# Exponentials added on GpSimd, w_out converted in three places, and a second MLP layer that gives rows

## The chip, the cores and the metric

The kernel runs on one core of a Trainium2 chip. A core has five engines that work side by side and wait for one another by semaphores: TensorE (PE, matrix products, with its weight loads shown as PEld), VectorE (DVE), ScalarE (ACT), GpSimd (POOL) and SyncE (SP), which here issues most of the DMAs. The metric is device time in microseconds; the kernel before takes 1161.94 us (median of 3 runs, 1161.27 to 1163.94).

## The reference

Three layers follow each other, for 1792 tokens of width 768:

```
attention: 4 batches x 12 heads, 448 positions, head width 64, q and k RMS-normalised;
           exp(scores - row max) / (row sum + 1e-9) @ v
routing:   logits = x @ w_gate; all 1792 x 8 pairs in descending order; a token goes to the first
           expert that still has room (224 tokens each); out = relu(x @ w1[e]) @ w2[e]
MLP:       h = x @ w_in (768 -> 2048); out = (h * cos(h)) @ w_out (2048 -> 768)
```

`w_in` and `w_out` arrive as float64 in DRAM; the kernel turns each value into two float32 parts (hi and lo) so that three fast products (hi*hi, hi*lo, lo*hi) keep the accuracy.

## The kernel before

**A planner sets the order.** The code does not issue instructions. It adds steps (engine, estimated cost, reads, writes) to a plan; `Plan.run` then simulates the engines with these costs and emits each engine's instructions in the order it found. So the order on each engine is fixed at build time, and an engine waits at an instruction whose input is late, whatever stands behind it.

**Attention** works on 24 pairs of heads. For a pair, `scores` makes the transposed scores in four chunks of 112 keys and two heads, ACT takes the exponential into `pf` (112 x 448), `weigh` multiplies them with v (`po`) and sums them over the keys by products with a column of ones (`dn`, 32 columns wide, in full float32), 8 tiles times 4 column groups per pair. POOL does part of the normalisation (`qn`, `rt`, `rs`) and a small copy (`mx`).

**Conversion of w_in and w_out** (`Narrow.piece`) takes one DMA in, one ACT operation, four DVE operations, one more ACT and one more DVE operation, and one DMA out. There are 32 pieces of w_in (384 elements a partition) and 24 of w_out (512 elements). `EARLY = 48` of the 56 are placed as filler under attention; the last 8 are converted straight into the weight tiles of the first MLP (`fresh`).

**Experts and MLP.** The router finds, expert by expert, which 224 tokens it gets (`phase`; a long chain of small DVE operations). The tokens are gathered by an indirect DMA (`xr`), transposed, and go through `expert`; w1 and w2 are split into hi and lo by ACT and DVE as they arrive. After two experts, `mlp` runs on their 448 tokens: the first layer makes 16 tiles of 128 features (`acc`), a cosine of six operations follows, and leaves `gh` and `gl`. The second layer makes six tiles of 128 outputs: the weights are stationary, the 448 tokens are the moving operand, 16 x 3 products each. Its result is transposed, so each tile is copied by ACT (`o`), turned back by four PE transposes (`tr`), copied by DVE into `xo`, and at the end four indirect DMAs of 112 rows put the rows where the index tile `idx` says. There are four such groups; the last splits its last tile in two halves of 224 tokens.

Of the kernel before, what the change touches and what calls it, by code (L numbers as in the profile page):

```python
# [264 lines left out]
LAND = 7.0  # L265
# [4 lines left out]
class Narrow:  # L270

    WIDE = {"wi": 3, "wo": 4}

    def __init__(self, nc, pairs):

        self.nc = nc
        self.todo, self.at = [], {}
        for tag, src, dst in pairs:
            s = src.bitcast(I32)
            for f in range(dst.shape[0]):  # L280
                n = self.WIDE[tag]
                for k in range(0, dst.shape[2], n):
                    w = s[k * 128:(k + n) * 128, f * 256:(f + 1) * 256].rearrange("(k p) c -> p k c", p=128)
                    self.at[tag, f, k] = len(self.todo)
                    self.todo.append((w, dst[f, :, k:k + n], f"{tag}{f}:{k}"))

    def piece(self, plan, i, raw, mag, parts=None):
# [3 lines left out]
        n = dst.shape[1]  # L291
        r, a = raw[:, 0:n], mag[:, 0:n]
# [3 lines left out]
        plan.add([("SP", 0.46, lambda: nc.sync.dma_start(r, src))], [], [r], dma=0.36 * n, land=LAND)  # L296
# [7 lines left out]
        plan.add([("SP", 0.46, lambda: nc.sync.dma_start(dst, o.bitcast(F32)))], [o], [name], dma=0.36 * n)  # L304

    def plan(self, plan, pool, last):

        most = max(self.WIDE.values())
        raw = plan.ring(pool)("nr", 4, [128, most, 256], I32)
        mag = plan.ring(pool)("na", 2, [128, most, 128], I32)  # L310
        for i in range(last):
            self.piece(plan, i, raw(), mag())
# [20 lines left out]
NKQ = 5  # L333
XKA = 0
# [20 lines left out]
def attention(tc, P, R, ident, q, k, v, g_q, g_k, w_gate, x_dram, L, other):  # L355
# [4 lines left out]
    with ExitStack() as ctx:  # L360
# [27 lines left out]
        pfs = ring("pf", NPF, [CP + 1, S])  # L388
# [40 lines left out]
        P.rush, pw = -1000.0, bd()  # L429
# [22 lines left out]
        for _ in range(NPF):  # L452
            zset(pfs()[96:CP + 1], 1.0)
# [87 lines left out]
        def scores(P_, a, z):  # L541

            k, q, t = keys[P_ % NKQ], queries[P_ % NKQ], shift_rows[P_ % 4]
            for c in range(a, z):
# [14 lines left out]
                for h in range(2):  # L559
                    pf = exps[P_, h, c] = pfs()  # L560
                    sc.activation(pf[0:CP], ps[h], AF.Exp)

        outs = {}

        def weigh(P_):
# [5 lines left out]
            for c0 in range(0, NC, 2):  # L571
                def both():
                    for c in range(c0, c0 + 2):
                        for h in range(2):
                            pe.matmul(po[h * D:(h + 1) * D], t[:, h, c], exps[P_, h, c][0:CP], start=c == 0,
                                      stop=c == NC - 1)

                block(both)
# [146 lines left out]
class Router:  # L725
# [3 lines left out]
    def __init__(self, nc, pool, ident, L, rows):  # L729
# [76 lines left out]
        v.tensor_copy(io, tmp[0:CP, 272:272 + CP])  # L806
        pc = t("pc", [CP, NCOL, 3], BF16)
# [237 lines left out]
    def phase(self, idx, eid, first, quick):  # L1045
# [52 lines left out]
        nc.rush = rush  # L1098

# [18 lines left out]

CP, E, CAP, DM, F1, F2 = 112, 8, 224, 768, 1024, 2048
# [10 lines left out]
TURN = 5  # L1130
# [5 lines left out]
def moe(tc, P, R, ident, x_rows, w1, w2, w_in, w_out, out, narrow):  # L1136

    nc = tc.nc
    with ExitStack() as ctx:
# [10 lines left out]
        rbuf = ring("r", 3, [128, PT])  # L1150
        kbuf = ring("k", 2, [128, PT], I32)
        obuf = ring("o", 1, [128, PT])
# [3 lines left out]
        xf = cst.tile([128, KD, CAP], F32, name="xf")  # L1156
        xo = cst.tile([CP, 4, DM], F32, name="xo")
        mags = ring("na", MAGS, [128, 4, 128], I32)
        x2h = cst.tile([128, KD, PT], F32R, name="x2h")
        x2l = cst.tile([128, KD, PT], F32R, name="x2l")  # L1160
        gh = cst.tile([128, K2, PT], F32R, name="gh")
        hT = gh[:, K1:K2]
        gl = cst.tile([128, K2, PT], F32R, name="gl")
# [5 lines left out]
        def route(t, behind):  # L1169
# [3 lines left out]
            R.phase(idx[t], eid[t], t == 0, t in QUICK)  # L1173
# [62 lines left out]
        def ready(src, k0, n, keys):  # L1236

            x = parts()[:, 0:n]
            P.add([("SP", 0.46, lambda: nc.sync.dma_start(x.bitcast(F32), src[:, k0:k0 + n]))], keys, [x],
                  dma=n * 0.35)  # L1240
            return x[:, :, 0], x[:, :, 1]

        def fresh(d, k0):
            x = parts()
            for k in range(k0, k0 + K1, 4):
                i = narrow.at["wo", d, k]
                if i >= EARLY:
                    raw = stage().rearrange("p k n -> p (k n)").bitcast(I32).rearrange("p (k n) -> p k n", k=4)
                    narrow.piece(P, i, raw, mags(), x[:, k - k0:k - k0 + 4])
# [54 lines left out]
        def mlp(grp, ahead):  # L1304
            w = len(grp) * CAP
            for f in range(K2):
                hi, lo = ready(w_in[f], 0, KD, [f"wi{f}:{k}" for k in range(0, KD, narrow.WIDE["wi"])])
                p = acc()[:, 0:w]
                for d in range(KD):
                    block(lambda: three(p, hi[:, d], lo[:, d], x2h[:, d, 0:w], x2l[:, d, 0:w], d == 0, d == KD - 1))  # L1310
                r, k, a = rbuf()[:, 0:w], kbuf()[:, 0:w], gh[:, f, 0:w]
# [7 lines left out]
                P.either("tensor_tensor", gl[:, f, 0:w], r, a.bitcast(F32), op=ALU.subtract)  # L1319
            for d in range(KD):  # L1320
                if grp is GROUPS[0] and narrow.at["wo", d, 0] >= EARLY:
                    both = [fresh(d, k0) for k0 in range(0, K2, K1)]
                else:
                    both = [ready(w_out[d], k0, K1, [f"wo{d}:{k}" for k in range(k0, k0 + K1, narrow.WIDE["wo"])])
                            for k0 in range(0, K2, K1)]
                last = d == KD - 1
                if d == TURN:
                    ahead()
                cut = w // 2 if last and grp is GROUPS[-1] else w
                for a in range(0, w, cut):  # L1330
                    n, z = cut // CP, slice(a, a + cut)
                    p = acc()[:, 0:cut]
                    for f in range(K2):
                        hi, lo = (x[:, f % K1] for x in both[f // K1])
                        block(lambda: three(p, hi, lo, gh[:, f, z], gl[:, f, z], f == 0, f == K2 - 1))
# [4 lines left out]
                    g0 = a // CP  # L1340
                    v.tensor_copy(xo[:, g0:g0 + n, d * 128:(d + 1) * 128],
                                  q[0:CP, 0:n * 128].rearrange("p (g c) -> p g c", g=n))
                    for g in range(g0, g0 + n) if last else ():
                        P.add([("POOL", 1.07, lambda g=g: scatter(xo[:, g], idx[grp[g // 2]][:, g % 2:g % 2 + 1]))],
                              [xo[:, g]], [], dma=0.96)
# [20 lines left out]

        fetch(0)
        for grp in GROUPS:
# [4 lines left out]
            behind = chain[-EARLIER]  # L1373
            mlp(grp, lambda: fetch(grp[-1] + 1, behind))
        P.run(zip(chain, chain[1:]), *TUNE_B)

EARLY = 48
# [3 lines left out]
def kernel(  # L1381
# [22 lines left out]
    w_out32 = dram.tile([KD, 128, F2 // 128, 2, 128], F32, name="w_out32")  # L1404
    narrow = Narrow(nc, [("wi", w_in, w_in32), ("wo", w_out, w_out32)])
# [35 lines left out]
```

## Time and profile before

| | |
|---|---|
| median of 3 runs | 1161.94 us |
| the profiled execution | 1161.31 us, of which the span is 1159.4 us |
| mean granted clock | 0.976 |
| PE, DVE, ACT, POOL busy | 96%, 77%, 56%, 12% |
| attention's last PE work | about 348 us into the span |
| first expert's first product | 384.8 us |

PE's busy time includes modelled ends of pipelined products, so it is not a measure of how full PE is. The rate is read from the starts of successive products, and which engine limits a stretch from its busy share there.

### The profile page before, as it was taken

To read this page: it belongs to the slowest core of one execution; us is meant where nothing else is said; L and a number is where in the kernel's file an instruction comes from. 1 tells how busy PE (TensorE), PEld (TensorE's weight loads), DVE (VectorE), ACT (ScalarE), POOL (GpSimd) and SP (SyncE) were. 2 spreads that over 40 slices of the span, in tenths; PEclk is the share of its full clock that TensorE was granted. 3 is DMA by queue.
4 is the path that set the end of the run, shared out by engine and by line. 5 is a ranking of instruction groups with operands and counts; after the bars stand their busy time and mean duration, and the time that the engine had idled before them with its cause. 6 is when DMAs were issued, how large, how long until landed. Compare 5 with 4: busy or idle time off the path is not lost.

```text
span 1159.4 us, 22182 instructions
## 1 busy us (share of the span) xinstructions
PE 1107.4 (96%) x7944; PEld 912.5 (79%) x7944; DVE 895.6 (77%) x2477; ACT 646.0 (56%) x1575; POOL 134.2 (12%) x288
## 2 busy tenths in 40 slices
PE   7999999999994999999999999999999999999996
PEld 4556666665553888999898899899899889999996
DVE  7878999999958888996997887578789577856401
ACT  4867888866552456763456564246666235746400
POOL 5432432331000000000001000001000000100001
PEclk9989999999995899999999999999999999999998
DMA  7236476565641489779579568838866956856761
GB/s 215 81 115 207 150 251 204 172 221 203 218 171 50 129 229 293 239 257 293 209 185 263 203 218 248 297 115 239 244 216 222 301 194 174 238 205 218 245 218 48
DMA packets 180814, 237.58 MB, mean 205 GB/s; under 512 B 14112, under 2 KB 156896, under 8 KB 175072
## 3 DMA queue, kind: packets, MB, share of 16 engines
q1 hardware_dynamic: 178144, 225.15, 61.4%
q0 software_dynamic: 2560, 11.01, 3.6%
q8 instruction: 62, 1.02, 0.4%
q14 instruction: 48, 0.39, 0.1%
HBM read 199.52 MB, written 36.52 MB: 204 GB/s over the span
## 4 chain that ended last, share of the span: by engine, by line
PE 36%; DVE 7%; DMA 6%; issue 1%; ACT 1%; SPq 0%; POOL 0%; POOLq 0%; ACTq 0%; DVEq 0%
PE acc L47 35%; DMA ws<-in_moe_w_dram 4%; DMA wx<-w_out 2%; DVE wx L47 2%; PE tr L47 1%; DVE r L47 1%; DVE oh L47 1%; ACT wx L1231 1%; DVE na L47 1%; DVE xo L47 0%; SPq L1014 0%; DMA rows<-vm 0%; DVE gl L47 0%; DVE xe L47 0%; POOL out_dram L1351 0%
## 5 line engine op out<-in xcount | busy, mean ns | idle before, releaser
L47 PE MATMUL acc<-gh,wx 128*128 128x448 f32 (+1 forms) x1568 | 360.7, 344 | 4.9 <-DVE gh L47 3.7
L47 PEld LDWEIGHTS acc<-gh,wx 128*128 128x128 f32 x1568 | 264.5, 189 | 23.5 <-DVE gh L47 6.0
L47 PE MATMUL acc<-x2h,wx 128*128 128x448 f32 x768 | 222.4, 368 | 0.0
L47 PEld LDWEIGHTS acc<-x2h,wx 128*128 128x128 f32 x768 | 144.7, 188 | 11.0
L47 PE MATMUL acc<-gl,wx 128*128 128x448 f32 (+1 forms) x400 | 143.2, 358 | 0.0
L47 PE MATMUL acc<-x2l,wx 128*128 128x448 f32 x384 | 140.3, 365 | 0.0
L47 DVE TENSOR_TENSOR wx<-ws,wx 128x768 fp32r<-128x768 f32 (+1 forms) x104 | 112.3, 1080 | 24.3 <-ACT wx L1231 22.1
L47 ACT ACTIVATE pf<-st 112x448 f32<-112x448 f32 x192 | 93.9, 539 | 50.4 <-PE st L47 49.8
L1231 ACT ACTIVATE wx<-ws 128x768 fp32r<-128x768 f32 (+1 forms) x104 | 97.7, 940 | 25.9 <-DMA ws<-in_moe_w_dram 14.0
L47 DVE TENSOR_REDUCE cm<-s 128x1 f32<-128x448 f32 x168 | 99.6, 618 | 12.5 <-PE s L47 10.1
L47 PE MATMUL acc<-xe,wx 128*128 128x448 f32 (+1 forms) x672 | 107.1, 320 | 0.5 <-DVE wx L47 0.5
L47 ACT ACTIVATE r<-r 128x448 f32<-128x448 f32 x128 | 74.1, 579 | 57.8 <-DVE r L47 56.0
L47 PEld LDWEIGHTS acc<-xe,wx 128*128 128x128 f32 x672 | 100.8, 189 | 5.4 <-DVE wx L47 0.8
L47 PE MATMUL st<-qq,kk 64*112 64x448 f32 x576 | 91.5, 397 | 1.9 <-ACT pf L47 1.9
L47 ACT ACTIVATE oh<-oh 128x896 bf16<-128x896 bf16 x48 | 45.6, 950 | 74.6 <-DVE oh L47 74.5
L1182 POOL DMA_INDIRECT xr<-x,idx x16 | 15.6, 977 | 588.1 <-issue 198.2
L47 PE MATMUL po<-pf,vr 112*64 112x448 f32 x384 | 83.1, 552 | 0.0
L47 PEld LDWEIGHTS acc<-gl,wx 128*128 128x128 f32 x400 | 75.5, 189 | 4.7
L47 PEld LDWEIGHTS acc<-x2l,wx 128*128 128x128 f32 x384 | 72.3, 188 | 5.2
L47 PEld LDWEIGHTS st<-qq,kk 64*112 64x112 f32 x576 | 49.3, 175 | 31.8 <-ACT pf L47 9.8
L47 ACT ACTIVATE sq<-qk 112x64 f32<-112x64 f32 (+1 forms) x195 | 57.2, 301 | 8.4 <-DVE rt L47 4.6
L47 DVE COPY xo<-tr 112x512 f32<-112x512 f32 (+1 forms) x25 | 16.6, 666 | 58.1 <-PE tr L47 56.4
(251 smaller groups left out, 1830.8 us busy)
## 6 DMA issues: line engine op xcount, KB each, us to landing
wx<-w_in SPq DMA_DIRECT2D x64, 768.0 KB
wx<-w_out SPq DMA_DIRECT2D x44, 1024.0 KB
ws<-in_moe_w_dram SPq DMA_DIRECT2D x64, 384.0 KB
ws<-in_moe_w_dram SPq DMA_DIRECT2D x48, 512.0 KB
nr<-in_moe_w_in_dram SPq DMA_DIRECT2D x32, 384.0 KB
w_in<-nr SPq DMA_DIRECT2D x32, 384.0 KB
nr<-in_moe_w_out_dram SPq DMA_DIRECT2D x16, 512.0 KB
w_out<-nr SPq DMA_DIRECT2D x16, 512.0 KB
```

Source lines behind the costliest of these rows:

```text
L47: self.plan.add([(self.eng, self.plan.cost(self.eng, name, out, r, kw), lambda: f(*args, **kw), self.plan.shares(self.eng, name, out, r, k ...
L1182: P.add([("POOL", 2.1 - 0.9 * h, lambda x=x, h=h: nc.gpsimd.indirect_dma_start(out=x, out_offset=None, in_=x_rows, in_offset=bass.Indirect ...
L1231: P.add([("ACT", 0.093 + n * 0.1067, lambda: nc.scalar.activation(hi, s, AF.Copy)), ("DVE", 0.07 + n * 0.0667, lambda: nc.vector.tensor_co ...
```

## The change

- After each pair of exponentials, POOL adds two neighbouring chunks into a new tile `pa`; the sums then use two tiles instead of four for each head. For the last pair only the first two chunks are added.
- `w_out` is stored in two layouts: 8 blocks of 256 rows by 512 columns, and 4 blocks of 512 rows by 256 columns. 38 pieces are converted under attention (`EARLY`), 6 after the first gather (`GAP`), into memory that is used later (`r`, `xo`), and 12 in the first MLP: the second half of every one of the 12 blocks. The first halves are loaded back from DRAM.
- The second layer has the tokens (`gh`, `gl`) as stationary operand, 128 at a time, and the weights as moving operand, 512 and then 256 columns wide. A group has 448 tokens; the first and third group do three tiles of 128 and leave 64 tokens, the second and fourth do four tiles with these 64. All three or four accumulators of a group are open at once. The result comes as rows: ACT writes it into `xo`, without transposes, and three or four indirect DMAs of 128 rows send it off.
- `place` moves the row indices into this division by products with a shifted identity.

```diff
-                    self.at[tag, f, k] = len(self.todo)
...
+                    tile = (b + 8 * (tag == "wo1")) % 3 if i else -1
+                    self.todo.append(((tag != "wi") * (1 + (i > 0) + (tile > 0)), (tag, b, i), (
+                        w.rearrange("(k p) c -> p k c", p=128), dst[b, :, i:i + n], f"{tag}{b}:{i}")))
+        self.todo.sort(key=lambda t: t[0])
...
+        def halved(P_, c):
+            if c and P_ == NPR - 1:
+                return
+            for h in range(2):
+                a = exps[P_, h, -1 - c] = pas()
+                P.gpsimd.tensor_tensor(a[0:CP], exps[P_, h, c], exps[P_, h, c + 1], op=ALU.add)
...
-                    for c in range(NC):
-                        n, e = CP + (c == 0), exps.pop((P_, h, c))
+                    halves = [c for c in (0, 2) if (P_, h, -1 - c) in exps]
+                    for c in range(0, NC, 2) if len(halves) == 2 else (0, 2, 3):
+                        n, e = CP + (c == 0), exps.pop((P_, h, -1 - c if c in halves else c))
...
-            for d in range(KD):
-                if grp is GROUPS[0] and narrow.at["wo", d, 0] >= EARLY:
-                    both = [fresh(d, k0) for k0 in range(0, K2, K1)]
...
-                    o, q = obuf()[:, 0:cut], turn()
-                    sc.activation(o, p, AF.Copy, scale=-1.0)
-                    for g in range(n):
-                        P.tensor.transpose(q[0:CP, g * 128:(g + 1) * 128], o[:, g * CP:(g + 1) * CP], ident)
...
+            starts, c0 = range(o, REST + PT - 64 * (1 - g % 2), 128), 0
+            for z, w in enumerate(w_out):
+                n, m = w.shape[2], w.shape[4]
+                ps = [acc()[:, 0:m] for _ in starts]
+                for k in range(0, K2, n):
+                    tag, b = f"wo{z}", k // n
+                    if g == 0 and narrow.late(tag, b, EARLY + GAP):
+                        hi, lo = fresh(w[b], tag, b)
+                    else:
+                        hi, lo = ready(w[b], narrow.keys(tag, b))
+                    if z and k == TURN:
+                        ahead()
+                    for s, p in zip(starts, ps):
+                        for i in range(n):
+                            f = k + i
+                            a, b = gh[:, f, s:s + 128], gl[:, f, s:s + 128]
...
+                                P.tensor.matmul(p, a, hi[:, i], start=f == 0, stop=False)
+                                P.tensor.matmul(p, b, hi[:, i], start=False, stop=False)
+                                P.tensor.matmul(p, a, lo[:, i], start=False, stop=f == K2 - 1)
...
         fetch(0)
+        gather = next(t for t in P.steps[n:] if t.ways[0][0] == "POOL" and t.dma)
+        for i in range(EARLY, EARLY + GAP):
+            n = len(P.steps)
+            narrow.piece(P, i, raws(), mags())
+            P.steps[n + 1].after[gather] = True
...
-EARLY = 48
+EARLY = 38
+GAP = 6
```

On PE, in the middle of attention, the sums of a pair (`dn`, each row four products) stood directly behind the pair's second half of `po`:

```order
L47 MATMUL po_223<-pf_199,vr_165 64x448
L47 MATMUL po_223<-pf_200,vr_165 64x448
L47 MATMUL dn_224<-pf_193,ones 32x112 x4
L47 MATMUL dn_224<-pf_195,ones 32x112 x4
L47 MATMUL dn_224<-pf_197,ones 32x112 x4
L47 MATMUL dn_224<-pf_199,ones 32x112 x4
L47 MATMUL dn_224<-pf_194,ones 32x112 x4
L47 MATMUL dn_224<-pf_196,ones 32x112 x4
L47 MATMUL dn_224<-pf_198,ones 32x112 x4
L47 MATMUL dn_224<-pf_200,ones 32x112 x4
```

In the same place of the changed kernel a block of eight score products and one more stand between them:

```order
L47 MATMUL st_231<-qq_151,kk_146 112x448
L47 MATMUL st_230<-sr_158,heads 112x448
L47 MATMUL st_231<-sr_158,heads 112x448
L47 MATMUL s_229<-kk_147,qq_152 128x448
L47 MATMUL dn_233<-pa_210,ones 32x112 x4
L47 MATMUL dn_233<-pa_206,ones 32x112 x4
L47 MATMUL dn_233<-pa_211,ones 32x112 x4
L47 MATMUL dn_233<-pa_207,ones 32x112 x4
L47 MATMUL dn_233<-xe_216,wg 32x112 x4
```

The sums are half as many and come later by about one block of scores.

On DVE, near the end of the first MLP, the changed kernel's conversions (`na`, and `wx` for their last step) stand among the cosine (`r`, `gl`) and the routing (`row`, `w`, `rp`):

```order
L47 TENSOR_TENSOR wx_4239<-na_4248,wx_4239 128x512
L47 SCALAR_TENSOR_TENSOR na_4249<-ws_4232,na_4249 128x512
L47 TENSOR_SCALAR na_4250<-na_4250 128x512
L47 CAST dg_4259<-rt_4230 112x6
L47 TENSOR_SCALAR na_4247<-na_4247 128x512
L47 SCALAR_TENSOR_TENSOR na_4250<-ws_4233,na_4250 128x512
L47 TENSOR_TENSOR wx_4236<-na_4249,wx_4236 128x512
L47 SCALAR_TENSOR_TENSOR na_4250<-ws_4233,na_4250 128x512
L47 TENSOR_SCALAR na_4247<-na_4247 128x512
L47 TENSOR_TENSOR gl<-r,gh 128x448
L47 TENSOR_TENSOR wx_4237<-na_4250,wx_4237 128x512
```

Before, the corresponding stretch had the cosine behind it and mixed 8 conversions with the next router phase:

```order
L47 TENSOR_TENSOR wx_4608<-na_4626,wx_4608 128x4x128
L47 TENSOR_TENSOR wx_4609<-na_4627,wx_4609 128x4x128
L47 TENSOR_SCALAR ti<-rt_4603 128x1
L47 TENSOR_TENSOR KX<-KX,ti 128x1
L47 TENSOR_TENSOR b<-KX,ix 128x1
L47 TENSOR_SCALAR oh<-AB,b 128x896
L47 SCALAR_TENSOR_TENSOR oh,cnt<-AB,b,one 128x896
L47 TENSOR_SCALAR na_4625<-na_4625 128x512
```

Four more conversions now stand between the first cosine and the first weights of the third expert.

On SP, before the first expert's second layer, its first weights (`ws`, eight blocks) stood directly behind those of the first layer:

```order
L1222 DMA ws_4606<-in_moe_w_dram 128x6x128
L1222 ISA
L1222 DMA ws_4607<-in_moe_w_dram 128x6x128
L1222 ISA
L1222 DMA ws_4604<-in_moe_w_dram 128x8x128
```

Now the store of the first piece of the gap stands between:

```order
L1267 DMA ws_4234<-in_moe_w_dram 128x6x128
L1267 ISA
L1267 DMA ws_4235<-in_moe_w_dram 128x6x128
L317 DMA w_out_68<-r 128x1024
L1267 ISA
L1267 DMA ws_4232<-in_moe_w_dram 128x8x128
```

The load behind it can't be issued until DVE has finished that piece.

## Rows read from the trace of the kernel before

**Rows 1.** The page: busy us, share of the span and instructions of each engine.

```profile
PE 1107.4 (96%) x7944; PEld 912.5 (79%) x7944; DVE 895.6 (77%) x2477; ACT 646.0 (56%) x1575; POOL 134.2 (12%) x288
```

**Rows 2.** Stretches: length, busy PE, PEld, DVE, ACT, POOL; clock; DMA share, GB/s.

```profile
197.20:275.20 78.00, 77.58 (x861) 47.35 (x858) 74.08 (x192) 57.37 (x158) 23.05 (x48) 1.00 0.61 204
275.20:349.10 73.90, 68.83 (x783) 40.07 (x782) 59.77 (x153) 42.47 (x93) 4.46 (x8) 1.00 0.55 187
...
375.90:424.00 48.10, 44.69 (x283) 41.26 (x282) 41.12 (x202) 21.84 (x56) 4.49 (x6) 0.88 0.64 180
424.00:471.40 47.40, 46.34 (x277) 42.53 (x276) 39.53 (x88) 32.29 (x66) 0.00 (x0) 1.00 0.97 264
471.40:498.10 26.70, 26.70 (x135) 24.09 (x134) 25.77 (x58) 18.39 (x36) 0.00 (x0) 1.00 0.70 236
498.10:568.30 70.20, 70.20 (x368) 63.74 (x367) 58.95 (x172) 32.69 (x60) 2.09 (x2) 1.00 0.80 265
568.30:585.00 16.70, 16.33 (x96) 14.31 (x94) 14.89 (x43) 7.28 (x13) 0.00 (x0) 1.00 0.45 143
```

**Rows 3.** The second layers of the four groups, instructions on acc alone.

```profile
520.30:585.00 64.70, 61.52 (x291) 53.30 (x290) 1.85 (x3) 3.20 (x6) 1.00 0.72 236
710.40:775.30 64.90, 61.94 (x289) 52.73 (x287) 1.85 (x3) 3.27 (x6) 1.00 0.70 219
899.70:965.20 65.50, 61.95 (x290) 52.79 (x288) 1.84 (x3) 3.27 (x6) 1.00 0.70 217
1086.40:1148.10 61.70, 60.91 (x337) 56.11 (x335) 1.53 (x3) 3.62 (x7) 1.00 0.47 158
```

**Rows 4.** Timeline of PE, a pair's sums: start, us, instruction.

```profile
335.95 1.75 PE L47 MATMUL dn<-pf,ones 113*32 113x112 f32 x64
337.52 0.38 PE L47 MATMUL dn<-xe,wg 128*32 128x112 f32 x8
```

**Rows 5.** Stretches, conversions (tile na) alone: length, DVE busy, clock, DMA.

```profile
60.00:340.00 280.00, 112.87 (x232) 0.98 0.60 198
376.00:585.00 209.00, 22.11 (x40) 0.97 0.76 232
```

**Rows 6.** Tile nr: duration ns least, median, most; first and last start.

```profile
L47 DVE TENSOR_TENSOR nr<-na,nr x48: 543/558/1447, 61.8 to 336.5; 128x384 fp32r<-128x384 f32 x32, 128x512 fp32r<-128x512 f32 x16
```

**Rows 7.** Timeline of POOL and DVE, two places in attention.

```profile
117.87 1.99 POOL L47 TENSOR_TENSOR rt<-rs 112x48 f32<-112x48 f32 x1 [0.88 <-DVE rs L47]
...
128.34 1.04 POOL L47 TENSOR_TENSOR qn<-qk,rs 112x512 f32<-112x512 f32 x1
128.72 1.55 DVE L47 TENSOR_TENSOR nr<-na,nr 128x384 fp32r<-128x384 f32 x2
```

**Rows 8.** POOL's groups by form: busy us, mean ns, idle before.

```profile
L47 POOL TENSOR_TENSOR qn<-qk,rs 112x512 f32<-112x512 f32 x42 | 43.7, 1043 | 133.9 <-PE t L47 115.6 <-issue 17.3
```

**Rows 9.** Timeline of PE, second layer of the fourth group.

```profile
1095.72 0.37 PE L47 MATMUL acc<-gl,wx 128*128 128x448 f32 x1
...
1098.15 0.37 PE L47 MATMUL acc<-gl,wx 128*128 128x448 f32 x1
```

**Rows 10.** Chain that ended last, fourth group's last two half tiles.

```profile
1139.07 0.44 PE tr L47 x4
1139.51 2.68 PE acc L47 x24
```

**Rows 11.** Groups by form: a weight load and the copy of a turned tile.

```profile
L47 PEld LDWEIGHTS acc<-gh,wx 128*128 128x128 f32 x1568 | 264.5, 189 | 23.5 <-DVE gh L47 6.0 <-DMA wx<-w_out 1.5 <-DVE wx L47 0.9
...
L47 DVE COPY xo<-tr 112x512 f32<-112x512 f32 x23 | 15.8, 687 | 57.7 <-PE tr L47 56.0 <-PE rt L47 1.7
```

**Rows 12.** Timeline of POOL at the end: the first and last of four stores.

```profile
1149.09 0.94 POOL L1351 DMA_INDIRECT out_dram<-xo,idx  x1 [150.13 <-DVE xo L47]
...
1152.82 0.94 POOL L1351 DMA_INDIRECT out_dram<-xo,idx  x1 [0.22 <-issue]
```

**Rows 13.** Timeline of POOL: the gather for the fourth expert.

```profile
596.65 0.93 POOL L1182 DMA_INDIRECT xr<-x,idx  x1 [63.49 <-DVE sm L47]
```

More of the change, by code (lines that the diff above doesn't have):

```diff
@@ L333 @@
 NKQ = 5
+NPA = 6
 XKA = 0
@@ L451, in attention @@
             zset(ones[0:CP, j, j:j + 1], 1.0)
-        for _ in range(NPF):
-            zset(pfs()[96:CP + 1], 1.0)
+        for _ in range(NPA):
+            zset(pas()[96:CP + 1], 1.0)
         for t in mix:
@@ L1098, in phase @@
         nc.rush = rush
+        v.tensor_copy(digits, pi[0:CP, 0:6])
     def close(self):
@@ L1116, in close, with turns, take @@
         self.nc.rush += LATER
+def turns(*xs):
+    at = [0]
+    def take():
+        at[0] += 1
+        return xs[(at[0] - 1) % len(xs)]
+    return take
 CP, E, CAP, DM, F1, F2 = 112, 8, 224, 768, 1024, 2048
@@ L1129 @@
 AHEAD = 100.0
-TURN = 5
+TURN = 8
+REST = 64
 EARLIER = 140
@@ L1149, in moe @@
         parts = ring("wx", 4, [128, K1, 2, 128], F32R)
-        rbuf = ring("r", 3, [128, PT])
-        kbuf = ring("k", 2, [128, PT], I32)
-        obuf = ring("o", 1, [128, PT])
+        rk = cst.tile([128, 5 * PT], F32, name="r")
+        rbuf = turns(*(rk[:, i * PT:(i + 1) * PT] for i in range(3)))
+        kbuf = turns(*(rk[:, i * PT:(i + 1) * PT].bitcast(I32) for i in (3, 4)))
         sums = ring("sm", 2, [128, CAP])
@@ L1304, in mlp @@
         def mlp(grp, ahead):
[L1305 removed]
+            g = GROUPS.index(grp)
+            o = 0 if g % 2 else REST
             for f in range(K2):
[L1307 to L1308 removed]
+                hi, lo = ready(w_in[f], narrow.keys("wi", f))
+                p = acc()[:, 0:PT]
                 for d in range(KD):
[L1310 to L1311 removed]
+                    block(lambda: three(p, hi[:, d], lo[:, d], x2h[:, d], x2l[:, d], d == 0, d == KD - 1))
+                r, k, a = rbuf(), kbuf(), gh[:, f, o:o + PT]
                 sc.activation(k, p, AF.Copy, scale=1.0 / (2.0 * math.pi))
@@ new lines, in place @@
+        def place(grp):
+            g, p, move = GROUPS.index(grp), turn(), R.P["move"]
+            odd = g % 2
+            half = [digits[t % 4][:, 3 * h:3 * h + 3] for t in grp for h in range(2)]
+            if odd:
+                v.tensor_scalar(rest, digits[(grp[0] - 1) % 4][:, 3:6], R.P["tail"][0:CP], None, op0=ALU.mult)
+            P.begin()
+            for b in range(3 + odd):
+                parts = [(half[n], CP * n - 128 * b) for n in range(4) if -CP < CP * n - 128 * b < 128]
+                if b == 3:
+                    parts.append((rest, 16))
+                for x, o in parts:
+                    P.tensor.matmul(p[:, 3 * b:3 * b + 3], move[:, CP - o:CP - o + 128], x, start=x is parts[0][0],
+                                    stop=x is parts[-1][0])
+            P.finish()
+            n = 3 * odd
+            v.tensor_reduce(sum3[:, n:n + 3 + odd], p[:, 0:9 + 3 * odd].rearrange("p (b k) -> p b k", k=3), AX.X, ALU.add)
+            v.tensor_copy(to[:, n:n + 3 + odd], sum3[:, n:n + 3 + odd])
```

140 lines of the change are left out of this document (80 added, 60 removed).

## The prediction

> **What bounds the kernel now.** I read the page first. PE is busy for 96% of the span and DVE for 77% [rows 1]; PE's figure includes modelled ends, so it says little. Then I cut the span into stretches, from one landmark to the next in the timeline. In attention both are full: in the third batch of six pairs (78.0 us, 13.0 a pair) PE is busy for 77.6 and DVE for 74.1, that is 95%; in the fourth DVE falls to 59.8 of 73.9 [rows 2]. From the first index list (375.9) to the first converted weight of the third expert (568.3) DVE is busy for 41.12 + 39.53 + 25.77 + 58.95 = 165.4 of 192.4 us, 86%, with PE nearly without idle time [rows 2]. So in the first group PE sets the pace, and DVE has 27 us to spare. Third, the second layers by themselves: 64.7, 64.9, 65.5 and 61.7 us [rows 3]. Last, the end of the timeline, where four indirect stores follow each other after PE has finished [rows 12].
>
> **Attention.** Removed from PE: a pair's 32 sums are 64 instructions in the trace, which start from 335.95 on, and the next group starts at 337.52 [rows 4], so 1.57 us a pair. 23 pairs lose half (0.785 us), the last pair a quarter (0.39): 18.4 us. Removed from DVE: ten conversions of 512 elements. Eight such took 22.11 us [rows 5], 2.76 each, so 27.6 of the 112.9 us that conversions take there.
>
> Added: 94 additions of 112 x 448 on POOL. No row shows one. The nearest is the product `qn`, 112 x 512 in 1043 ns, whose second operand is small and repeated [rows 8]. By length alone an addition takes 0.91 us, the lower end; if the second full operand costs as much again, 1.83. I take 1.0, near the row: 94 us on an engine that was busy for 23 of 78 us in the third batch [rows 2]; four per pair make it 47. At 1.83 it would be 67 of 78, which still fits.
>
> POOL and DVE don't run freely beside each other. A `qn` starts at 128.34 and takes 1.04 us; two `nr` that begin on DVE at 128.72 take 1.55 together [rows 7], where the median of one is 0.558 and the longest 1.447 [rows 6]. The other way round, a tiny `rt` on POOL took 1.99 us at 117.87 [rows 7]. One waits for the other's end. The Trainium skill (SBUF — State Buffer, "Who interferes with whom") says the same and more: DVE instructions with two SBUF inputs and GpSimd instructions that read SBUF exclude each other for a whole instruction; the trace agrees with its 1.99 us. By that rule alone, with every meeting paid in full, the gain of attention could be nothing and the sum 1164; by the rows, which show single meetings, it is the sum below.
>
> What is left of the 18.4? About 38 x 5 conversions remain on DVE and can meet an addition. The sums also wait on PE now for two additions that start after the last exponential; the order puts one block of scores before them as cover, and behind a late sum PE's whole queue waits. If PE loses a quarter of a microsecond in each of 22 pairs, 5.4 us are lost. I take **-13** (ends: 0 if the two engines block each other, -18.4 if nothing is lost). Before the router's first list nothing of the change stands but one small cast: 0.
>
> **First group.** Six conversions come in after the first gather, and twelve instead of eight in the first MLP: 10 x 2.76 = 27.6 us more DVE work before the third expert's weights, 193.0 us instead of 165.4. Six copies of `xo` (0.687 us, [rows 11]) leave DVE, most of them behind that point. PE loses 10 us here (below), so DVE becomes the bound: at its old 86% it would take 224 us, at the 96.5% of its best stretch (25.77 of 26.70, [rows 2]) 200. I take 93%, as the pieces are work that can fill gaps: 207.5. The last conversion stands just ahead of the landmark, after which at most 30 narrow products (3.8 us) remain, some 2 us beyond it: 209.3, against 585.0 - 375.9 = 209.1. So PE's gain is gone and the group takes as long as before. On SP, store after store of converted pieces now waits for DVE ahead of expert weights, in a stretch where DMA is 97% busy [rows 2]; and the fourth expert's gather (596.65, 12 us after the MLP's end, [rows 13]) hangs on the same DVE queue. For both I add 4 us (0 to 10): **+4**.
>
> **Second layers.** Twelve products of 448 columns start between 1095.72 and 1098.15 [rows 9]: 202.5 ns each. 24 of 224 columns take 2.68 us [rows 10]: 111.7. The slope is 0.405 ns a column, so 512 columns take 229 to 231 (by proportion), 256 columns 124.7 to 128. I take 230 and 125, 355 ns a pair. Three tiles of tokens need 3 x 16 x 3 = 144 pairs, 51.1 us; four need 192, 68.2. Before: 288 products, 58.3 us, and 24 transposes at 0.44 per four [rows 10], 2.6; the remaining 3.7 to 4.6 us of 64.9 and 65.5 are router products, token transposes and waits, of which I keep 2.8, since the waits for `o`, `tr` and `xo` go.
>
> - Group 2: 68.2 + 2.8 = 71.0 against 64.9, +6.1. All four accumulators are needed within 4.1 us of the first layer's end, and the cosine of its last tile holds one; half a microsecond of wait is in the 2.8.
> - Group 3: 51.1 + 2.8 = 53.9 against 65.5, -11.6. Its 12.6 MB of weights (12 blocks of 128 x 2048 floats) then arrive in 54 us, 233 GB/s, under the 264 of [rows 2].
> - Group 4: 68.2 + 0.5 against 61.7, +7.0.
> - End: before, the first store starts at 1149.09 and the fourth at 1152.82 [rows 12]. Now the tiles end 12 x 0.125 = 1.5 us apart, more than the 1.24 between stores, so only one store is left after the last product: -3.8.
>
> `place` adds 7 to 12 tiny products a group and two DVE instructions, under 1 us in all, inside the 2.8.
>
> **Sum.** -13 + 4 + 6.1 - 11.6 + 7.0 - 3.8 = -11.3. The profiled execution took 1161.31 us, 0.6 under the median of the runs; 1161.3 - 11.3 = 1150.0. As the unknowns of the first group reach further up than down, I say **1151**.
>
> **Rivals.**
> 1. *Slower: DVE keeps its 86% in the first group.* Its operations hang on ACT and on one another, and a router chain can't be filled at will. Then the stretch takes 193.0 / 0.86 = 224.4, 15 us more than I forecast: 1166. It decides from a share of 88% down. For it: 86% is what it did over four stretches. Against: 96.5% where the cosine ran [rows 2], and 95% in attention.
> 2. *No change: attention gains nothing.* Additions block conversions and conversions block additions, DVE's key operations and PE's sums come late: -13 becomes 0, 1164. For it: the 1.99 us. Against: DVE has 27.6 us less to do, and much of its work in attention reads PSUM, which no row shows to wait.
> 3. *Much faster.* Attention gives all 18.4, DVE reaches 96.5% (200 + 2, so -7 instead of +4): 1151 - 5 - 11 = 1135.
> 4. *The narrow products run at the pace of weight loads*, 189 ns [rows 11]: 672 x 64 ns, +43, 1194. Against: the 224-column products at 111.7 ns with the same weight loads [rows 10].
>
> **How the numbers follow.** Forecast 0.60, rivals 0.14, 0.12, 0.10 and 0.04. The forecast's own range is 1140 to 1161. To hold 8 in 10 the whole range goes from 1137 to 1166, which takes in rivals 1 and 2 in part and leaves out 4 and most of 3. About 0.2% (2.3 us) is what can be told from no change. Faster: nearly all of the forecast (0.57), rival 3, a little of 1 and 2: 0.75. Same: 0.11, mostly rival 2. Slower: 0.14.
>
> **What would show it.** Additions near 1.0 us on POOL, and the last PE work of attention near 335 instead of 348; later than 343 speaks for rival 2. DVE's share from the first index list to the third expert's weights at 90% or more, and the first MLP's end 205 to 217 us after the list; 220 or more is rival 1. Second layers of some 71, 54 and 69 us in groups 2 to 4, and products of 256 columns 120 to 130 ns apart. One store after the last product. The forecast is wrong if the second layers are off by more than 3 us each, or if attention ends earlier but the router's list comes no earlier.

## The result and the profile after

The changed kernel takes 1143.23 us (median of 4 runs, 1141.23 to 1145.23) against 1161.61 for the kernel before in the same comparison: a ratio of 0.9854, with a 95% interval of 0.9831 to 0.9878. The forecast of 1151 was on the right side and 8 us too high. The profiled execution took 1143.85 us, its span 1141.7.

The page's line of engines is to be compared with [rows 1]. GpSimd has nearly twice the work, TensorE 28 us less:

```profile
PE 1079.2 (95%) x7268; PEld 875.2 (77%) x7268; DVE 899.2 (79%) x2472; ACT 646.4 (57%) x1578; POOL 253.7 (22%) x367
```

**Where the 17.7 us of span went.** The same landmarks, read from the timeline of TensorE in both traces, cut the program into stretches. A pair of heads ends with its part of the router's logits, the product that makes `dn` from `xe`.

| stretch | before | after | difference |
|---|---|---|---|
| start to the third pair's logits | 82.3 | 76.3 | -6.0 |
| third to last pair's logits | 264.9 | 251.5 | -13.4 |
| to the first expert's first product | 37.6 | 38.0 | +0.4 |
| first group, to the fourth expert's first product | 233.5 | 238.3 | +4.8 |
| the rest | 541.1 | 537.6 | -3.5 |

The rest splits into the second layers: from the first of their products to the next expert's first, group 2 went from 65.4 to 70.9 us, group 3 from 66.0 to 57.2; group 4, to TensorE's end, from 61.6 to 66.6; and what follows TensorE's end from 11.3 to 6.1.

The second layers' own instructions, in stretches of the changed kernel, are to be compared with [rows 3]. The columns are length, busy PE, PEld, DVE and ACT, clock, DMA share, GB/s; POOL has none here:

```profile
501.10:562.20 61.10, 53.79 (x289) 45.21 (x288) 2.45 (x4) 2.69 (x5) 0.97 0.88 288
695.00:765.80 70.80, 69.06 (x384) 58.85 (x383) 1.47 (x3) 4.00 (x8) 1.00 0.66 206
889.20:946.30 57.10, 53.38 (x288) 45.20 (x289) 1.84 (x3) 3.03 (x6) 0.97 0.75 249
1069.00:1135.70 66.70, 66.62 (x385) 58.82 (x383) 1.39 (x3) 4.13 (x9) 1.00 0.45 155
```

Groups 2 and 4 have 384 products, four tiles of tokens, and TensorE is busy with them almost throughout. Groups 1 and 3 have 288, and 4 to 7 us in which TensorE isn't busy with them. In group 1 the core moved 288 GB/s, and TensorE waited for converted weights, as the list of its waits from 501 to 605 us says (us in all, times, longest):

```profile
PE acc L47 <- DMA wx<-w_out: 5.2, 2, 3.4
PE rt L47 <- DVE pv L47: 4.7, 2, 4.5
PE tr L47 <- DMA xr<-x,idx: 1.4, 1, 1.4
```

The stretch from the first index list to the third expert's first converted weight has VectorE (the third busy time) busy for 190.26 of 202.90 us, 94%, where [rows 2] gave 86%:

```profile
356.50:559.40 202.90, 190.65 (x1107) 171.33 (x1106) 190.26 (x571) 120.44 (x241) 7.89 (x8) 0.97 0.83 264
```

The pace of the products stands in TensorE's timeline of group 4. Three products lie between two rows with `gl`, first 512 and then 256 columns wide:

```profile
1069.10 0.40 PE L47 MATMUL acc<-wx,gl 128*128 128x512 f32 x1
...
1069.79 0.39 PE L47 MATMUL acc<-wx,gl 128*128 128x512 f32 x1
...
1128.02 0.28 PE L47 MATMUL acc<-wx,gl 128*128 128x256 f32 x1
...
1128.38 0.28 PE L47 MATMUL acc<-wx,gl 128*128 128x256 f32 x1
```

That is 0.69 / 3 = 230 ns and 0.36 / 3 = 120 ns. GpSimd's timeline at the end is to be compared with [rows 12]; TensorE's last product starts at 1135.34, and one store is left:

```profile
1134.88 0.96 POOL L1429 DMA_INDIRECT out_dram<-xo,to  x1 [0.38 <-ACT xo L1397]
...
1136.32 0.96 POOL L1429 DMA_INDIRECT out_dram<-xo,to  x1 [0.39 <-ACT xo L1397]
```

The new additions, by tile (ns least, median, most; first and last start):

```profile
L47 POOL TENSOR_TENSOR pa<-pf,pf x94: 1130/1146/2343, 34.1 to 321.4; 112x448 f32<-112x448 f32 x94
```

### The profile page after: what moved, and what is told of

Read it like the earlier page. It is cut to its first block, busy times and chain, and to the rows that moved or that the text cites. A ratio compares the mean times of both kernels' runs of the same rounds, so it can differ in the third digit from the quotient of the medians.

```text
span 1141.7 us, 20959 instructions
## 1 busy us (share of the span) xinstructions
PE 1079.2 (95%) x7268; PEld 875.2 (77%) x7268; DVE 899.2 (79%) x2472; ACT 646.4 (57%) x1578; POOL 253.7 (22%) x367
## 4 chain that ended last, share of the span: by engine, by line
PE 37%; issue 14%; DVE 13%; DMA 6%; ACT 1%; POOL 1%; POOLq 0%; SPq 0%; DVEq 0%; ACTq 0%
PE acc L47 35%; DVE r L47 2%; DMA xr<-x,idx 2%; DVE oh L47 2%; DVE na L47 2%; DMA ws<-in_moe_w_dram 1%; DMA wx<-w_out 1%; DVE wx L47 1%; DVE AB L47 1%; DMA w_out<-wx 1%; PE rt L47 1%; PE tr L47 1%; DVE gl L47 1%; DMA ws<-in_moe_w_out_dram 0%; POOL xr L1227 0%
## 5 line engine op out<-in xcount | busy, mean ns | idle before, releaser
L47 PE MATMUL acc<-wx,gh 128*128 128x512 f32 (+1 forms) x896 | 228.5, 343 | 5.2 <-DMA wx<-w_out 5.2
L47 PEld LDWEIGHTS acc<-wx,gh 128*128 128x128 f32 x896 | 157.1, 192 | 24.6 <-DMA wx<-w_out 6.1
L47 PEld LDWEIGHTS acc<-x2h,wx 128*128 128x128 f32 x768 | 144.5, 188 | 11.3
L47 PE MATMUL acc<-wx,gl 128*128 128x512 f32 (+1 forms) x448 | 151.9, 339 | 0.0
L47 PE MATMUL acc<-gh,wx 128*128 128x448 f32 (+1 forms) x768 | 129.2, 325 | 3.8 <-DVE gh L47 1.3
L1227 POOL DMA_INDIRECT xr<-x,idx x16 | 19.0, 1189 | 506.0 <-issue 144.7
L47 POOL TENSOR_TENSOR pa<-pf,pf 112x448 f32<-112x448 f32 x94 | 113.5, 1228 | 71.8 <-ACT pf L47 71.7
L47 PEld LDWEIGHTS acc<-gh,wx 128*128 128x128 f32 x768 | 116.3, 191 | 11.2 <-ACT wx L1276 1.7
L47 DVE TENSOR_REDUCE cm<-s 128x1 f32<-128x448 f32 x168 | 100.3, 618 | 15.8 <-PE s L47 13.4
L47 DVE SCALAR_TENSOR_TENSOR r<-r,acc 128x448 f32<-128x448 int32 (+1 forms) x128 | 77.9, 618 | 31.8 <-ACT r L47 30.6
L47 PEld LDWEIGHTS acc<-wx,gl 128*128 128x128 f32 x448 | 85.8, 191 | 8.4
L47 PE MATMUL st<-qq,kk 64*112 64x448 f32 x576 | 87.8, 389 | 0.6 <-ACT pf L47 0.5
L47 PE MATMUL po<-pf,vr 112*64 112x448 f32 x384 | 83.6, 552 | 0.0
```

What stands on the lines that cost most here:

```text
L47: self.plan.add([(self.eng, self.plan.cost(self.eng, name, out, r, kw), lambda: f(*args, **kw), self.plan.shares(self.eng, name, out, r, k ...
L1227: P.add([("POOL", 2.1 - 0.9 * h, lambda x=x, h=h: nc.gpsimd.indirect_dma_start(out=x, out_offset=None, in_=x_rows, in_offset=bass.Indirect ...
```

## The experiments

Four questions: is attention's gain from the halved sums, from the ten conversions, or from both? What do the additions cost? What took 6 us off the start? And why is the third expert late? Each run has one profiled execution. The stretch from the third to the last pair was 251.5 us in one run of the changed kernel and 251.7 in another. Between kernels with the same work in attention it differs more: the three with 48 conversions and no additions (the kernel before and those of experiments 4 and 5) have 264.9, 266.5 and 262.8 us. So a difference of up to 4 us between two kernels shows nothing by itself.

**1. The additions alone.** In the kernel before, only this, with `halved` as in the change and the tiles `pa` that it writes:

```diff
+            halved(P_, a)
...
-                    for c in range(NC):
+                    halves = [c for c in (0, 2) if (P_, h, -1 - c) in exps]
+                    for c in range(0, NC, 2) if len(halves) == 2 else (0, 2, 3):
```

> The kernel before with the additions of exponentials alone: all 48 conversions stay under attention, second layers as before. Theory A (TensorE sets attention's pace, so the halved sums are worth their 18.4 us by themselves, whatever VectorE has to do): last logits at 329 to 332 us instead of 347.2, time 1143 to 1147. Theory B (VectorE is full too, and the gain of 19.4 us in attention needed both edits): last logits at 338 to 344, time 1152 to 1158. Theory C (additions and conversions block each other): last logits at 346 or later, time 1160 or more.

Measured: 1190.21 us (ratio 1.0254, 1.0208 to 1.0301), last logits at 364.2. Theory C by the place and the time: alone, this part of the change makes the kernel 30 us slower. The stretch from the third to the last pair is 16.9 us longer. Another 6.8 us go between the last logits and the first expert: the last step `nr` of a conversion now starts at 374.7, behind the logits, where the kernel before had it at 336.5 ([rows 6]). The first group and the rest take 2 and 4 us more.

**2. The change without the additions** (the lines of experiment 1 taken out of the changed kernel):

```diff
-            halved(P_, a)
...
-                    halves = [c for c in (0, 2) if (P_, h, -1 - c) in exps]
-                    for c in range(0, NC, 2) if len(halves) == 2 else (0, 2, 3):
+                    for c in range(NC):
```

> The changed kernel without the additions: the sums run over four tiles a head, as before; 38 conversions under attention, six after the first gather, twelve in the first MLP, second layers giving rows. Theory A: last logits at 344 to 347 us (TensorE has its 18.4 us back), and the rest of the program gives about +1.7 as in the changed kernel, so 1159 to 1163. Theory B: ten conversions less are worth something by themselves, last logits at 337 to 342, time 1151 to 1157.

Measured: 1151.22 us (0.9927, 0.9901 to 0.9953), last logits at 336.4, close to theory B. Of these 10.8 us, 4.9 lie before the third pair (experiment 5). From the third to the last pair it is 5.9 us less than in the kernel before, and 3.8 to 7.5 less than in the three kernels with 48 conversions and no additions. So ten conversions less give attention some time by themselves, though TensorE has its 18.4 us back: VectorE did limit it, which theory A denied.

The stretch from the third to the last pair in both runs (length, busy PE, PEld, DVE, ACT, POOL; clock; DMA share, GB/s), the additions alone first:

```profile
82.40:364.20 281.80, 258.50 (x2273) 146.11 (x2267) 258.88 (x595) 190.24 (x559) 178.03 (x211) 0.97 0.57 181
```

and the change without additions:

```profile
77.40:336.40 259.00, 256.94 (x2930) 157.10 (x2926) 213.01 (x549) 181.73 (x537) 57.12 (x116) 1.00 0.52 166
```

The kernel before, and the changed kernel behind it:

```profile
82.30:347.20 264.90, 260.09 (x2931) 157.56 (x2925) 236.95 (x600) 192.03 (x560) 59.92 (x116) 1.00 0.60 200
```

```profile
76.30:327.80 251.50, 244.95 (x2285) 141.59 (x2278) 232.22 (x564) 184.17 (x558) 173.98 (x213) 1.00 0.52 168
```

Read VectorE's column. Moving the conversions takes it from 236.95 to 213.01 us (-23.9; the sum had 27.6 for all of attention). The additions put 21.9 us on it with 48 conversions (258.88) and 19.2 with 38 (232.22), although the change gives VectorE no instruction for them: its operations get longer. (Of the 19.2, some 5 us are 15 instructions more that fall between the two landmarks, 564 for 549. Experiment 3 compares at equal counts.) With 48 conversions VectorE is busy for 92% of a stretch that has grown; with 38 it has back what the additions take, and TensorE's shorter work shows.

Two of VectorE's operations show which ones get longer, from 76 to 330 us (count | busy us, mean ns | idle time before), in the kernel before

```profile
L47 DVE SCALAR_TENSOR_TENSOR na<-nr,na 128x384 int32<-128x384 int32 x60 | 31.9, 566 | 0.2
L47 DVE TENSOR_REDUCE cm<-s 128x1 f32<-128x448 f32 x133 | 79.0, 618 | 8.3 <-PE s L47 6.4
```

and with the additions alone:

```profile
L47 DVE SCALAR_TENSOR_TENSOR na<-nr,na 128x384 int32<-128x384 int32 x60 | 38.0, 669 | 0.0
L47 DVE TENSOR_REDUCE cm<-s 128x1 f32<-128x448 f32 x128 | 75.5, 614 | 12.2 <-PE s L47 11.2
```

A conversion's step with two operands in SBUF goes from 566 to 669 ns on average; the maximum `cm`, which reads the scores in PSUM, stays at 618 and 614. A tiny operation on one tile, `t<-K`, gets longer too, from 166 to 377.

The Trainium skill (SBUF — State Buffer, "Who interferes with whom") says that VectorE instructions with two inputs in SBUF contend with GpSimd instructions that read SBUF. The trace agrees with it in these four rows.

**3. Short additions.** The order on every engine stays. In both kernels an addition takes 16 of 448 columns and leaves the others as they were:

```diff
-                P.gpsimd.tensor_tensor(a[0:CP], exps[P_, h, c], exps[P_, h, c + 1], op=ALU.add)
+                P.add([("POOL", 0.1 + S * 0.00217, lambda a=a, x=x, y=y: nc.gpsimd.tensor_tensor(
+                    a[0:CP, 0:16], x[:, 0:16], y[:, 0:16], op=ALU.add), True)], [x, y], [a[0:CP]])
```

> As the run with the additions alone (1190.2 us; last logits at 364.2), every instruction in the same place on its engine, but each addition takes in 16 of the 448 columns, so that GpSimd holds for some 0.15 us instead of 1.13; the sums are therefore not the right ones. Theory D (the durations: additions and VectorE's conversions keep each other out, and with 48 conversions VectorE has no time to give): last logits at 328 to 336 us, time 1143 to 1153. Theory E (the order: the sums wait for additions that stand late, and the planner placed the conversions badly): last logits at 352 or later, time 1175 or more.

> The changed kernel (1143.2 us; last logits at 327.8), every instruction in the same place, each addition over 16 of 448 columns (the sums are not the right ones). It prices the additions where VectorE has ten conversions less. Theory D: the last logits come at 318 to 324 us and the time is 1133 to 1140. If ten conversions less are enough room for the additions: last logits at 326 to 328, time 1141 to 1144.

Measured: 1165.17 us (1.0038, 1.0017 to 1.0059) with 48 conversions, last logits at 343.7; 1143.33 us (0.9843, 0.9819 to 0.9867) with 38, last logits at 323.2. The stretch with 48:

```profile
77.20:343.70 266.50, 255.45 (x2279) 145.37 (x2271) 236.91 (x595) 190.77 (x559) 86.91 (x210) 0.97 0.60 192
```

and with 38:

```profile
74.90:323.20 248.30, 244.27 (x2289) 141.83 (x2280) 221.26 (x564) 183.69 (x559) 83.97 (x211) 1.00 0.53 170
```

At equal counts of VectorE's instructions, the full length of the additions is worth 258.88 - 236.91 = 22.0 us of its busy time with 48 conversions and 232.22 - 221.26 = 11.0 with 38.

With 48 the durations cost 281.8 - 266.5 = 15.3 us of the stretch, so theory D has the larger part of it. But the stretch doesn't fall below the 262.8 to 266.5 of the kernels without additions: half the sums bring nothing here even when additions are nearly free. That was in neither theory (343.7 and 1165 lie between D and E). The likely reason is VectorE, with 237 us of work and 89% of the stretch as in the kernel before, but this isn't shown. The order is the one that was planned for long additions, which is what was left of theory E, and TensorE is busy for 11 us more than with 38 conversions, on as many products, at a mean granted clock of 0.97 instead of 1.00. A kernel planned anew for short additions was not run.

With 38 the price in the stretch is only 3.2 us. By its place (323.2) this run fits theory D, by its time (1143.33) the alternative, as the 3.2 us don't reach the end: the first group takes 242.8 us instead of 238.3, and its fourth expert starts at 603.8, hardly earlier than in the changed kernel (604.1). Why the group takes back what attention gains stays open.

**4. The second layers alone**, with the changed word of experiment 5. The changed kernel without additions, and

```diff
-EARLY = 38
-GAP = 6
+EARLY = 48
+GAP = 0
```

> The changed kernel without additions and with 48 conversions under attention, none after the gather and eight of w_out's second halves in the first MLP: of the change, the second layers that give rows, alone. By the traces of before and after, groups 2 to 4 and the end should give +5.5 -8.7 +5.0 -5.2 = -3.4 us, the first group's second layer -3.2, attention 0 (last logits at 345 to 348): time 1153 to 1157. A rival: rows bring nothing by themselves, because what the third group saves is given back before the next first layer: 1159 to 1162.

Measured: 1140.78 us (0.9833, 0.9817 to 0.9850), 12 us under the expectation and at least as fast as the whole change. Attention is that of the kernel before (third to last pair 266.5 us). The start has the same 6 us as in the changed kernel (third pair at 76.4), which the expectation didn't have. The first group takes 224.0 us, 9.6 less than before, where 3.2 were expected: its second layer has three tiles, as in group 3, and with only eight conversions there nothing takes that back. What follows the first group takes 534.5 us, 3.1 less than in the changed kernel. So additions and moved conversions together gained 266.5 - 251.5 = 15.0 us in attention and lost 238.3 - 224.0 = 14.3 in the first group.

**5. The start.** The kernel before, with one word of the diff:

```diff
-        P.rush, pw = -1000.0, bd()
+        P.rush, pw = -1000.0, bo()
```

> The kernel before with one word changed: the products that keep TensorE warm at the start go to an accumulator of po's ring instead of dn's. In the traces of all kernels with the new second layers and no additions the second to fourth pair come 4.3 to 6 us earlier than before, and the granted clock from 60 to 80 us is 1.00 instead of 0.74. If this word does that (it moves where the sums of the first two pairs stand): last logits at 342 to 344 us instead of 347.2, time 1155 to 1158. If something else in the change does it: last logits at 346 to 348, time 1160 to 1162.

Measured: 1157.01 us (0.9961, 0.9945 to 0.9977), 4.2 us less; the third pair at 76.7 instead of 82.3. The stretch from 60 to 80 us, first of the kernel before, then with the other bank:

```profile
60.00:80.00 20.00, 17.22 (x95) 9.99 (x89) 15.65 (x36) 11.45 (x39) 9.21 (x20) 0.74 0.36 117
```

```profile
60.00:80.00 20.00, 18.70 (x183) 11.21 (x181) 17.76 (x43) 16.92 (x62) 10.29 (x20) 1.00 0.39 127
```

The clock, behind the five busy times, is 0.74 against 1.00. In the kernel before, the warm-up products take a bank of `dn`'s ring, and the sums of the first two pairs are both done late, from 56 to 60 us; TensorE then waits five times between 57.8 and 63.8, the last time longest (its timeline):

```profile
63.82 0.46 PE L47 MATMUL t<-ident,dn 128*112 128x128 f32 x1 [0.88 <-DVE qq L47]
```

and from there it runs below full clock (0.62 from 63.0 to 76.3). With the word changed two waits are left between 57 and 68 us, 0.51 and 0.30 us, and the clock stays at 1.00 over the same 13.3 us. Between these two kernels the place of the buffer is shown to be the cause; that the clock, not the waits themselves, makes up most of the 4.2 us is read from these rows, not tried. The last logits came at 339.5, earlier than expected, and of these 7.7 us 3.8 are lost again after the fourth expert's start, where the word changes nothing.

The word is not the only thing that decides. The kernel of experiment 3 with 48 conversions has the old bank, and yet its third pair comes at 77.2 and its clock from 60 to 80 us is 1.00; with long additions (experiment 1) these are 82.4 and 0.83. The changed kernel with the old bank was not run, so that the word makes up its 6 us as well is likely, not shown.

**6. More conversions under attention.** The changed kernel with `EARLY = 44`, once with `GAP = 6` (six are left for the first MLP) and once with `GAP = 0` (twelve are left):

```diff
-EARLY = 38
+EARLY = 44
```

> The changed kernel with six more conversions under attention (44 instead of 38), six after the first gather, and six instead of twelve in the first MLP. VectorE gets 6 x 2.76 = 16.6 us more in attention and as much less in the first MLP. If the third expert waits for VectorE (its router list comes behind twelve conversions), its 41.9 us shrink to 34 to 37; if its wait has another cause, they stay at 41 to 42. If attention has room on VectorE, last logits come at 328 to 331, and the time is 1135 to 1140; if VectorE is attention's bound, they come at 335 to 342, and the time is 1142 to 1152.

> The changed kernel with the six conversions of the gap moved into attention (44 there, none after the gather, twelve in the first MLP). It has the same attention as the run with 44 and 6, so last logits within 1 us of that one. If the conversions of the first MLP alone delay the third expert, it keeps its 41 to 42 us and the first group gains only what the gap's stores cost (0 to 3 us); if VectorE's whole work since the first list counts, 16.6 us less of it give the same gain as in the run with 44 and 6 (third expert 34 to 37 us).

Measured: 1150.56 us (0.9923, 0.9887 to 0.9959) and 1156.51 us (0.9959, 0.9931 to 0.9987). The third to the last pair take 271.0 and 270.2 us, so six conversions, 16.6 us of work, cost 19 there: more than was expected even of a full VectorE (last logits at 349.6 and 346.6, not at 335 to 342). The row of the first:

```profile
78.60:349.60 271.00, 254.40 (x2281) 146.86 (x2277) 254.15 (x586) 189.46 (x568) 173.91 (x213) 0.97 0.55 177
```

The third expert takes 33.1 us with six conversions in the first MLP and 39.9 with twelve (41.9 in the changed kernel). Both kernels have twelve conversions after the list in all, so VectorE's whole work since the list doesn't explain the 39.9; twelve in the first MLP are enough to make this expert late. In the changed kernel the wait stands in TensorE's timeline, at the router's product and at the gather behind it:

```profile
584.80 1.56 PE L47 MATMUL rt<-pv,oh 112*112 112x6 bf16 x16 [4.54 <-DVE pv L47]
...
598.79 0.61 PE L47 MATMUL tr<-ident,xr 112*128 112x112 f32 x4 [1.41 <-DMA xr<-x,idx]
```

**7. Twelve in the gap.** The changed kernel with

```diff
-GAP = 6
+GAP = 12
```

> The changed kernel with twelve instead of six conversions after the first gather and six instead of twelve in the first MLP; attention as in the changed kernel (last logits at 327 to 329). If the third expert is late because twelve conversions of the first MLP stand on VectorE between the router's operations, it takes 34 to 36 us instead of 41.9; the first two experts get 0 to 6 us longer for it, as VectorE's work from the first list on is the same: 1136 to 1143. If VectorE's whole work is what counts, the gain and the loss are alike and the time is 1143 to 1147.

Measured: 1158.94 us (0.9988, 0.9970 to 1.0006); a miss. The third expert is still at 39.9 us with only six conversions in the first MLP, so their number there isn't the whole cause either: it is late with twelve in the first MLP or with 18 after the list, and in time with six in the first MLP and twelve after the list. The first two experts together take 83.6 us instead of 75.5, and the first layer of the first MLP takes 74.1 us instead of 59.8. TensorE's waits from 368 to 530 us name the gathered rows, the converted w_in and the cosine:

```profile
PE tr L47 <- DMA xr<-x,idx: 4.2, 2, 3.9
PE acc L47 <- DMA wx<-w_in: 4.2, 2, 3.9
PE acc L47 <- DVE r L47: 4.1, 3, 2.0
PE acc L47 <- DVE gh L47: 2.8, 1, 2.8
```

The gap is no empty place: six more pieces there make the experts and the first layer beside them longer. Which of the waits costs how much was not tried.

**8. Additions where VectorE has room.** Two kernels with `EARLY = 44`, `GAP = 6`: one without additions, one with them for the first 12 of 24 pairs, and the changed kernel beside them on the same chip.

```diff
-            if c and P_ == NPR - 1:
+            if P_ >= 12:
                 return
...
-                    for c in range(0, NC, 2) if len(halves) == 2 else (0, 2, 3):
+                    for c in range(0, NC, 2) if len(halves) == 2 else range(NC):
```

> The changed kernel without additions, with 44 conversions under attention, six after the gather and six in the first MLP. If what additions and moved conversions do to each other was the loss, this lies near the run with the rows alone (1140.8): last logits at 339 to 343 us, first group 224 to 227 us from its first expert to the second group's second, time 1137 to 1142. If the gap's pieces cost what they cost with 12 in the first MLP: 1145 to 1150.

> As the run without additions and 44 conversions, with additions for the first 12 of 24 pairs only: there TensorE loses 12 x 0.785 = 9.4 us, and the conversions that VectorE can't do there find room in the last pairs, where it is idle without additions. If room on VectorE over the whole of attention decides: last logits at 332 to 337 us, time 1131 to 1137. If additions push conversions back one for one (theory D at its full price): last logits at 339 to 345, time 1138 to 1146.

> The changed kernel on the same chip as the three others, for the comparison: 1141 to 1145 us. If the run with the rows alone is really the faster one, the run without additions and 44 conversions is at least 2 us below it.

Measured: 1149.91 us (0.9892, 0.9871 to 0.9913) without, 1136.97 us (0.9784, 0.9763 to 0.9805) with half of the additions, and 1146.29 us (0.9870, 0.9843 to 0.9897) for the changed kernel, 1.3 above its expectation: the mixture beats both kernels, at the upper end of the first range expected (last logits at 335.6). Its stretch:

```profile
75.00:335.60 260.60, 253.52 (x2649) 150.27 (x2641) 239.13 (x598) 191.22 (x567) 110.59 (x166) 1.00 0.59 190
```

That is 3.3 us less than without additions (263.9), no more than such stretches differ among themselves. VectorE is busy for 67.4 of the 80 us from 270 on, without additions for 61.2, so it does have more left to do in the last pairs, as expected. The larger part of its lead lies at the start: its third pair came at 75.0 us, that of the run without additions at 81.9. The run without additions missed its expectation by 8 us, and it isn't faster than the changed kernel: besides that late start its first group took 229.1 us, not 224 to 227. Why its start is late stays open; in its profile TensorE waits 3.5 us there for the small DMA of `sr`, in the changed kernel 3.2 without the same effect.

**All together.** The stretch from the third to the last pair by the number of conversions and of pairs with additions over all 448 columns, in us:

| conversions under attention | no additions | additions for 12 pairs | for all pairs |
|---|---|---|---|
| 38 | 259.0 | | 251.5, 251.7 |
| 44 | 263.9 | 260.6 | 271.0, 270.2 |
| 48 | 264.9, 266.5, 262.8 | | 281.8 |

The additions with the halved sums gain 7.5 us with 38 conversions and cost 15 to 19 with 48. Ten conversions cost 4 to 7.5 us without additions and 30 with them. So neither edit has a price of its own; the gap between the two is several times what like kernels differ by.

## Why the prediction was right, step by step

- **What bounds the kernel.** Right that both engines are full in attention. Wrong in the conclusion that TensorE's 18.4 us are worth most of themselves: with 48 conversions they brought nothing, even with short additions (experiment 3). They count because the same change takes 24 us from VectorE, of which the additions use up most (19.2).
- **Attention, -13.** The term covered everything to the last logits, which came 19.4 us earlier, beyond its end of -18.4. From the third to the last pair it was -13.4. That this meets the -13 is partly luck: the sum was 18.4 less 5.4 for waits, and what the runs show is 5.9 for the moved conversions and 7.5 for the additions with the halved sums, each with a price that hangs on the other. The failed step is the start, which had no term: the one-word change of the bank was in the diff and was passed over, while the start gave -6.0 (the word by itself, in the kernel before: -4.2 in the medians). That is most of the 8 us by which the forecast was high.
- **One addition, 1.0 us.** Median 1.146, least 1.130: between the bounds, nearer to the lower one.
- **Rival 2 (they block each other).** Its mechanism is there: 22 us on VectorE with 48 conversions, 11 with 38 (experiment 3). It would have decided had the conversions stayed (experiment 1). The sum priced the meetings at 5.4 us and the conversions as hidden room.
- **First list, 0.** From the last logits to the first expert it was +0.4.
- **First group, +4.** Measured +4.8. VectorE's share from the first list to the third expert's weights was to be 93% of 207.5 us and is 94% of 202.9, so rival 1 is out. By its third expert's start the group had gained 3.6 us; that expert then took 8.3 us longer (experiments 6 and 7), about twice the 4 us set aside for stores and gather. So this term, too, is right partly by luck: two errors of some 4 us cancel.
- **Second layers.** The sum had 355 ns for a pair of products; 230 + 120 = 350, and 120 lies below the 124.7 to 128 that it worked out. Group 2 +5.5 for +6.1, group 4 +5.0 for +7.0, group 3 -8.7 for -11.6: it has 57.2 us for 50.4 of products, more waits than the 2.8 us left for them (2.25 at one gather). The end -5.2 for -3.8, with one store left as said. Together -3.4 for -2.3.
- **Rival 4** is out by the 120 ns. One difference in the prediction is off: the remainder of the old second layers is 4.0 to 4.6 us by its own numbers, not 3.7 to 4.6. Nothing hangs on it.

Without the start, the terms sum to -11.3 as predicted and -11.7 as measured. The forecast's middle was right, but "attention gains, the first group is even" hid that two of the three edits nearly cancel (15.0 us gained, 14.3 lost); that needed experiment 4.

## What to carry to other kernels

When two engines are full in a stretch, work taken from one can be worth nothing until the other is relieved as well; here the same edit gained 7.5 us or cost 15 to 19, by what else VectorE had to do. GpSimd work beside VectorE counts on VectorE's account: look for added time in the durations of instructions that the change doesn't touch. Read a diff to its last word, as the choice of a buffer for warm-up products was worth 4.2 us in the kernel before, against 18.4 for this whole change. Work that is moved out of a full stretch arrives in another; price both ends before adding up, and try half of the change too.

## What the runs showed of the hardware

A GpSimd addition with two full operands in SBUF took 1.13 us at least for 448 columns, 2.5 ns a column, against 1.04 us for 512 columns with a small repeated operand ([rows 8]). A stretch of short waits early in the program (five of 0.28 to 0.88 us within 6 us) was followed by 13 us at a mean granted clock of 0.62, that is, partly on the lower level of 1.2 GHz; with two waits of 0.51 and 0.30 us in their place it ran at 1.00. With 128 x 128 weights loaded for each product, 256 columns still came every 120 ns, though a weight load lasted 190.
